# Exponentials of four key tiles computed during the MLP and kept in HBM, maxima by one matmul a unit, w2 re-read per chunk

## The chip, the cores and the metric

The kernel runs on one core of one Trainium2 chip. The metric is the device time of one launch, in microseconds; the median of several runs is given, and beside it one execution with the hardware profiler, whose trace is read below. The engines are named as in the profile: PE (TensorE matmuls), PEld (its weight loads), DVE (VectorE), ACT (ScalarE), POOL (GpSimd), SP (SyncE, which here only issues DMAs).

## The reference

One transformer block in parallel form, for 2048 tokens of width 448, all in float32:

```python
xn = layernorm(x)                                   # S, D = 2048, 448
# A: 16 query heads of 28, one shared key and value head
q = (xn @ wq).reshape(S, 16, 28);  k = xn @ wk;  v = xn @ wv
p = softmax(einsum("qhd,kd->hqk", q, k) * 28 ** -0.5)
A = einsum("hqk,kd->qhd", p, v).reshape(S, 448) @ wo
# B: a second layer norm, then an MLP of width 1792
h = gelu(layernorm(xn) @ w1 + b1)                   # tanh form
B = h @ w2 + b2
out = x + A + B
```

## The kernel before

Tokens are taken in 4 chunks of 512 (CW). Projections and MLP work in pairs of fp32r halves: a value is split into a high part and a rest, and three products (high by high, high by rest, rest by high) are added in PSUM.

The kernel has three stages, in one order that is written out by hand (each engine and each DMA queue runs its instructions in that order). 

Stage 1 (`norm_parts`, `q_slot`, `v_slot`): both layer norms, transposes of x, and the projections. Queries go to HBM, a high part in `qd[0]` and the rest in `qd[1]`, as rows of 512 tokens (L407); keys stay in SBUF as `ks` (four blocks of 32 partitions, the high part and the rest twice each). A few of the keys are also kept as `kz`, 32 keys per block.

Stage 2, the MLP: 4 chunks of 14 slots (`mlp1(c, ft)` and, two slots behind, `mlp2`). `mlp1` runs 11 matmuls into a PSUM bank `ph`, then ACT and DVE compute gelu in five instructions (L567 to L571), and the result is split by DVE and POOL into `hh` and `hl`. `mlp2` runs 12 matmuls of 448 columns into four banks (L586). Both halves of w2 (`w2h`, `w2l`) are made in the first chunk and stay in SBUF. MLP results plus x and b2 go to HBM as `ad`.

Stage 3, attention: 16 units, each one of 4 chunks by one of 4 groups of 4 heads. `load_q` brings a unit's queries into a tile `qst` (blocks of 28 partitions). `max_jobs` takes each query's largest score over 32 keys (16 matmuls of 128 columns, 4 DVE reductions, a transpose, and two small DMAs that write the negated maximum into rows 60 and 124 of the query tile, where `ks` holds ones, so that the score matmul subtracts it). Then a unit has 8 steps of two key tiles:

```python
            for i, (kt, h) in enumerate(((k, h) for k in (2 * step, 2 * step + 1) for h in range(2))):
                scores(u, kt, h)
...
            for v, kt in waiting:
                pv(v, kt)
```

`scores` (L697, L699) is a pair of matmuls of 128 keys by 512 queries for two heads into a two-bank tile `s` (three of them), and one exponential of 1024 columns into `p`. `pv` (L706) multiplies the weights `p` by the values, for four heads in four column strips of PE, one step behind the scores. `norm_jobs` normalises a finished unit, with small DMAs through HBM; `o_jobs` multiplies a finished chunk by wo (12 matmuls in each of four steps, L663 to L665) and writes the output. `last_norm` ends the last unit. If a sum of weights lies outside wide limits, a branch at the end recomputes attention with exact maxima; it is not taken here.

SP issues nearly all DMAs, and in program order: a DMA that waits for a semaphore holds those behind it.

Of the kernel before, what the change touches and what calls it, by code (L numbers as in the profile page):

```python
# [18 lines left out]
P = 128  # L19
S, D, H, DH, F = 2048, 448, 16, 28, 1792  # L20
NT = S // P
CT = 4
# [10 lines left out]
PAIRS = 14  # L33
# [4 lines left out]
def block_kernel(ctx, tc, x, wq, wk, wv, wo, w1, b1, w2, b2, out):  # L38
# [18 lines left out]
    qd = [dram.tile([D, S], F32, name=f"qd{i}") for i in range(2)]  # L57

    ks = keep.tile([P, S], F32R, name="ks")
    kz = keep.tile([P, P], F32R, name="kz")  # L60
# [76 lines left out]
    pool.memset(f(kz), 0.0)  # L137
# [231 lines left out]

    def w2_split(s):  # L370
        raw = wl_q.pop(0)
        ab = slice(2 * s, 2 * s + 2)

        act.activation(w2h[:, ab, :], raw, AF.Copy, scale=0.5)
        dve.scalar_tensor_tensor(w2l[:, ab, :], raw, 0.5, f(w2h[:, ab, :]), op0=ALU.mult, op1=ALU.subtract)  # L375
        if s + 2 < NF // 2:
            w2_load(s + 2)

    def q_slot(c, i):
        xh, xl = xts[c, False]  # L380
        cols = slice(c * CW, (c + 1) * CW)
        ms = slice(i * P, (i + 1) * P)
        ps = qpp.tile([P, CW], F32, name="qp")
        for cs in (slice(0, CW // 2), slice(CW // 2, CW)) if c < 2 and i == 0 else (slice(0, CW),):
            proj(ps, lambda b: wah[:, b, ms], lambda b: wal[:, b, ms], xh, xl, cs)

        def evac():
            qe = wqp.tile([P, 2, CW], F32R, name="qe", bufs=5)
            if c in KEPT:
                dve.tensor_mul(ps, ps, ibs[c])  # L390
            act.activation(qe[:, 0, :], ps, AF.Copy)
            vt = None
            if i == 0:
                vt = wqp.tile([32, CW], F32, name="vt", bufs=1)
                act.activation(vt, ps[0:32, :], AF.Copy)

            def low():
                dve.tensor_sub(qe[:, 1, :], ps, f(qe[:, 0, :]))  # L398
                if i == 0:
                    for dst, j in ((32, 0), (0, 1), (64, 1), (96, 0)):  # L400
                        nc.sync.dma_start(f(ks[dst:dst + DH, cols]), f(qe[32:60, j, :]))
                        if c == 0:
                            nc.sync.dma_start(f(kz[dst:dst + DH, :]), f(qe[32:60, j, 0:P]))
                at = slice(64 if i == 0 else 0, P)
                rows = slice(0, 64) if i == 0 else slice(i * P - 64, i * P + 64)
                for j in range(2):
                    nc.sync.dma_start(qd[j][rows, cols], f(qe[at, j, :]))  # L407
            return vt, low
        return evac
# [105 lines left out]
    def load_q(u, blocks=range(4)):  # L515
        c, g = units[u]
        qs = qss[u] = qst[u % 2]
        for b in blocks:
            blk, i = ((1, 0), (2, 0), (0, 1), (3, 1))[b]
            src = qd[i][4 * DH * g:4 * DH * (g + 1), c * CW:(c + 1) * CW].rearrange("(j r) n -> r j n", r=DH)  # L520
            nc.sync.dma_start(f(qs[32 * blk:32 * blk + DH]), src)

    def max_jobs(u, whole=False):
        qs = qss[u]
        mr = keep.tile([P, 4 * CT], F32, name="mr", bufs=2)
        for j in range(4):
            js = slice(CT * j, CT * j + CT)
            if whole:
                mx = keep.tile([P, CT, 4], F32, name="mx")
                for t in range(CT):  # L530
                    for n in range(4):
                        pm = bank([P, CW])
                        pe.matmul(pm, qs[:, j, t * P:(t + 1) * P], ks[:, n * CW:(n + 1) * CW], start=True, stop=True)
                        dve.tensor_reduce(mx[:, t, n:n + 1], pm, axis=AX.X, op=ALU.max)
                dve.tensor_reduce(mr[:, js], mx, axis=AX.X, op=ALU.max)
            else:
                pm = bank([P, CT, P])
                for t in range(CT):
                    pe.matmul(pm[:, t, :], qs[:, j, t * P:(t + 1) * P], kz, start=True, stop=True)  # L539
                dve.tensor_reduce(mr[:, js], pm, axis=AX.X, op=ALU.max)  # L540
            yield
        pm = bank([4 * CT, P])
        pe.transpose(pm, mr, ident)
        mn = keep.tile([4 * CT, 2, P], F32R, name="mn", bufs=2)
        dve.tensor_scalar(mn[:, 0, :], pm, -1.0, 0.0, op0=ALU.mult, op1=ALU.add)
        dve.scalar_tensor_tensor(mn[:, 1, :], pm, -1.0, f(mn[:, 0, :]), op0=ALU.mult, op1=ALU.subtract)
        for row, i in ((60, 0), (124, 1)):
            nc.sync.dma_start(f(qs[row:row + 1, :, :]), f(mn[:, i, :]))
        yield
# [5 lines left out]
    w2h = hp.tile([P, NF, D], F32R, name="w2h", bufs=1)  # L555
    w2l = hp.tile([P, NF, D], F32R, name="w2l", bufs=1)
# [3 lines left out]
    def mlp1(c, ft):  # L560
# [3 lines left out]
        proj(ph, lambda b: w1h[:, b, fs], lambda b: w1l[:, b, fs], yh, yl)  # L564
# [4 lines left out]
        dve.scalar_tensor_tensor(hz, hz, 1.0, hx, op0=ALU.add, op1=ALU.mult)  # L569
        act.activation(hz, hz, AF.Tanh, scale=GELU[1])  # L570
# [7 lines left out]
    def mlp2(c, ft):  # L578
# [4 lines left out]
        terms = ((hh, w2h), (hh, w2l), (hl, w2h))  # L583
        for k in range(CT):
            for i, (h, w) in enumerate(terms):
                pe.matmul(m2[k], h[:, k * P:(k + 1) * P], w[:, ft, :], start=(ft == 0 and i == 0),  # L586
                          stop=(ft == NF - 1 and i == 2))
            if ft == NF - 1:
                t = CT * MLP_ORDER[c] + k
                a = lines.pop(t)  # L590
                dve.tensor_add(a, a, m2[k])  # L591
                nc.sync.dma_start(ad[:, t, :], a)

# [6 lines left out]
    first_max = None  # L600
    for n in range(len(mslots) + 2):
        c, ft = mslots[n] if n < len(mslots) else (NCH, n - len(mslots))
        if 3 <= ft < 11 and ft % 2 and len(KEPT) <= c + 1 < NCH:
# [10 lines left out]
        if (c, ft) == (NCH - 1, 1):  # L614
            clear_q()
        if (c, ft) == (NCH - 1, 3):
            load_q(0)
            first_max = max_jobs(0)
        if n < len(mslots):
            mlp1(c, ft)  # L620
# [4 lines left out]
        if c == NCH - 1 and 6 <= ft < 11:  # L625
            next(first_max)
        if n >= 2:
            mlp2(*mslots[n - 2])
# [6 lines left out]
    clear_q()  # L635
# [66 lines left out]
    def pv(u, kt):  # L702
        if kt == 0:
            pos[u] = op.tile([P, CW], F32, name="po")
        for j in range(4):
            pe.matmul(pos[u][32 * j:32 * j + 32, :], vs[:, kt, :], ps[u, kt, j // 2][:, j % 2, :],  # L706
                      start=(kt == 0), stop=(kt == NT - 1))

    def last_norm(u, po):
# [5 lines left out]
        def blocks(t, h):  # L715
            return t[:, h].rearrange("p (a b) -> p a b", b=32)

# [3 lines left out]
        for i in range(2):  # L721
            h, r = slice(256 * i, 256 * i + 256), slice(8 * i, 8 * i + 8)
            dve.transpose(tr[:, h], po[:, h])
            dve.reciprocal(rc[:, r], blocks(tr, h)[:, :, 0])
            dve.transpose(blocks(rb, h), rc[:, r, None].to_broadcast([P, 8, 32]))
            dve.tensor_mul(on[:, h], po[:, h], rb[:, h])
            pool.tensor_copy(sums[:, u, r], blocks(tr, h)[:, :, 0])
# [9 lines left out]
    def at(u, step, g):  # L737
        side.setdefault((u, step), []).append(g)
# [4 lines left out]

    load_rows_of(0)
    waiting = []
    for u in range(NU):
        c, g = units[u]
        for step in range(NT // 2):
            if step == 0 and u + 1 < NU:
                load_q(u + 1)  # L750
                nexts = max_jobs(u + 1)
            for i, (kt, h) in enumerate(((k, h) for k in (2 * step, 2 * step + 1) for h in range(2))):
                scores(u, kt, h)
                if i == 0:
                    for job in side.pop((u, step), []):
                        next(job, None)
                if i == 1 and 2 <= step < 7 and u + 1 < NU:
                    next(nexts)
            for v, kt in waiting:
                pv(v, kt)  # L760
            if waiting and waiting[-1][1] == NT - 1:
                v = waiting[-1][0]
                job = norm_jobs(v, pos.pop(v))
                next(job)
                at(u, 2, job)
                at(u, 4, job)
                cv, gv = units[v]
                if gv == NG - 1:
                    outs = o_jobs(cv, range(NG))
                    for d in (6, 7, 8, 9):  # L770
                        at(u + d // 8, d % 8, outs)
                    at(u + 1, 2, rows_job(cv + 1))
                if v == NU - 2:
                    outs = o_jobs(NCH - 1, range(NG - 1))
                    for d in (5, 6, 7, 7):
                        at(u, d, outs)
            waiting = [(u, 2 * step), (u, 2 * step + 1)]
    for v, kt in waiting:
        pv(v, kt)
# [14 lines left out]
    with tc.If(outside > 0, preferred_fallthrough_block=False):  # L794
        for u in range(NU):
            c, g = units[u]
            pool.memset(f(qst[u % 2]), 0.0)
            load_q(u)
            for _ in max_jobs(u, True):
                pass  # L800
            for kt in range(NT):
                for h in range(2):
                    scores(u, kt, h)
                pv(u, kt)
# [29 lines left out]
```

## Time and profile before

| | |
|---|---|
| median of 3 runs | 975.1 us (974.23 to 975.5) |
| profiled execution | 976.61 us |
| its span, first to last instruction | 974.8 us |
| PE busy | 937.5 us (96%), 5181 matmuls |
| ACT busy | 645.3 us (66%) |
| DVE busy | 280.8 us (29%) |
| POOL busy | 154.8 us (16%) |
| DMA | 56.61 MB, mean 58 GB/s |
| first MLP matmul, last MLP matmul | about 66 us, about 352 us |
| attention | to about 960.6 us |

A busy PE is not PE at its peak, since matmuls are pipelined and each one's duration includes its passage through the array. Better measures are the spacing of starts and the chain of waits: the work that ended last, followed back from the last instruction, where each piece is shown with its start, its duration and what it was.

### The profile page before, as it was taken

The page shows a single profiled execution, that of the slowest core. Times are in us where ns is not written, and L with a number is a line of the kernel's source. Part 1 is how long each engine was busy: PE and PEld are TensorE (multiplying, and loading weights), DVE is VectorE, ACT ScalarE, POOL GpSimd, SP SyncE. Part 2 cuts the span into 40 slices and gives each one's busy share as a digit, 9 for nine tenths or more (in the row PEclk, how much of TensorE's full clock was granted, in tenths as well). Part 3 has the DMA queues.
Part 4 walks back from the last instruction along what each step waited for, and adds up shares of the span by engine and source line. Part 5 has one row for each costly group of instructions (what it writes and reads, how often), then busy time and mean ns, then how long its engine had stood idle before and what let it go on. Part 6 is the DMA issues. An engine that isn't in the chain of part 4 may idle for free.

```text
span 974.8 us, 13404 instructions
## 1 busy us (share of the span) xinstructions
PE 937.5 (96%) x5181; PEld 586.0 (60%) x5181; DVE 280.8 (29%) x539; ACT 645.3 (66%) x772; POOL 154.8 (16%) x149
## 2 busy tenths in 40 slices
PE   9999999999999979999999999999999999999995
PEld 8878888888888854444445644445644444644442
DVE  7855454353443431111102112111111112111003
ACT  6755443334443346888887688887688888588871
POOL 6434342342243320000000000000000000000000
PEclk9999999999999998999999999999999999999998
DMA  9771202002013050210210410210301201222001
GB/s 279 204 253 38 87 8 76 1 24 63 20 55 70 2 139 8 51 39 13 50 40 22 111 41 16 51 39 12 113 19 45 51 17 35 68 60 50 2 12 41
DMA packets 40256, 56.61 MB, mean 58 GB/s; under 512 B 10234, under 2 KB 26808, under 8 KB 40184
## 3 DMA queue, kind: packets, MB, share of 16 engines
q1 hardware_dynamic: 38776, 55.10, 20.1%
q8 instruction: 42, 0.69, 0.3%
q10 hardware_dynamic: 1408, 0.57, 0.2%
q14 instruction: 30, 0.25, 0.1%
HBM read 39.49 MB, written 14.80 MB: 56 GB/s over the span
## 4 chain that ended last, share of the span: by engine, by line
PE 87%; ACT 6%; DVE 2%; DMA 2%; issue 1%; POOL 0%; SPq 0%; ACTq 0%; DVEq 0%; POOLq 0%
PE po L706 24%; PE s L697 24%; PE m L586 13%; PE ph L173 11%; ACT p L699 5%; PE qp L173 3%; PE mo L539 3%; PE mo L665 1%; PE mo L663 1%; PE mo L664 1%; PE ph L178 1%; PE ph L176 1%; DMA xh<-qd 1%; DMA xl<-in_A_wo_dram 1%; PE qp L297 1%
## 5 line engine op out<-in xcount | busy, mean ns | idle before, releaser
L699 ACT ACTIVATE p<-s 128x1024 f32<-128x1024 f32 x512 | 484.6, 1029 | 127.0 <-PE s L697 127.0
L697 PE MATMUL s<-xh,ks 128*128 128x512 f32 x1024 | 308.9, 423 | 13.2 <-ACT p L699 10.9
L697 PEld LDWEIGHTS s<-xh,ks 128*128 128x128 f32 x1024 | 168.6, 189 | 176.0 <-ACT p L699 155.1
L706 PE MATMUL po<-p,vs 128*32 128x512 f32 x2048 | 247.7, 602 | 0.0
L706 PEld LDWEIGHTS po<-p,vs 128*32 128x32 f32 x2048 | 53.7, 109 | 124.6 <-issue 123.3
L567 ACT ACTIVATE hx<-ph,b1t 128x512 f32<-128x512 f32 x56 | 38.5, 688 | 117.3 <-PE ph L178 114.5
L689 POOL TENSOR_TENSOR otl<-oc,oth 128x512 fp32r<-128x512 f32 x15 | 19.2, 1280 | 559.1 <-DVE oth L688 559.1
L575 POOL TENSOR_TENSOR hl<-hx,hh 128x512 fp32r<-128x512 f32 x56 | 77.5, 1383 | 186.8 <-DVE hh L574 181.4
L540 DVE TENSOR_REDUCE mr<-mo 128x4 f32<-128x512 f32 x64 | 44.2, 691 | 201.4 <-PE mo L539 201.4
L586 PE MATMUL m<-w2l,hh 128*128 128x448 f32 x224 | 82.5, 368 | 0.9 <-DVE w2l L375 0.9
L586 PE MATMUL m<-w2h,hl 128*128 128x448 f32 x224 | 82.0, 366 | 1.0 <-POOL hl L575 1.0
L586 PE MATMUL m<-w2h,hh 128*128 128x448 f32 x224 | 82.4, 368 | 0.0
L569 DVE SCALAR_TENSOR_TENSOR hz<-hz,hx 128x512 f32<-128x512 f32 x56 | 44.5, 794 | 106.8 <-ACT hz L568 106.4
L173 PE MATMUL ph<-xh,w1h 128*128 128x512 f32 x168 | 66.1, 394 | 2.4 <-DVE qe L398 2.4
L570 ACT ACTIVATE hz<-hz 128x512 f32<-128x512 f32 x56 | 35.4, 632 | 48.3 <-DVE hz L569 48.3
L173 PE MATMUL ph<-xl,w1h 128*128 128x512 f32 x168 | 66.2, 394 | 0.0
L173 PE MATMUL ph<-xh,w1l 128*128 128x512 f32 x168 | 66.2, 394 | 0.0
L675 DVE COPY oc<-po 128x512 f32<-128x512 f32 x15 | 10.4, 692 | 146.6 <-PE po L706 146.6
L571 DVE SCALAR_TENSOR_TENSOR hx<-hz,hx 128x512 f32<-128x512 f32 x56 | 39.1, 699 | 43.6 <-ACT hz L570 43.6
L586 PEld LDWEIGHTS m<-w2l,hh 128*128 128x128 f32 x224 | 42.1, 188 | 7.2 <-DVE w2l L375 3.3
L539 PEld LDWEIGHTS mo<-kz,xh 128*128 128x128 f32 x256 | 38.7, 192 | 11.3 <-issue 5.6
L586 PEld LDWEIGHTS m<-w2h,hh 128*128 128x128 f32 x224 | 42.1, 188 | 4.9 <-DVE a L591 0.2
(148 smaller groups left out, 813.7 us busy)
## 6 DMA issues: line engine op xcount, KB each, us to landing
xh<-qd SPq DMA_DIRECT2D x64, 224.0 KB
qd<-qe SPq DMA_DIRECT2D x24, 256.0 KB
a<-in_A_x_dram SPq DMA_DIRECT2D x24, 224.0 KB
tr<-ld SPq DMA_DIRECT2D x60, 64.0 KB
ad<-a SPq DMA_DIRECT2D x16, 224.0 KB
a<-ad SPq DMA_DIRECT2D x16, 224.0 KB
raw<-in_B_w_dram SPq DMA_DIRECT2D x7, 448.0 KB
out_dram<-a SPq DMA_DIRECT2D x14, 224.0 KB
```

The lines of the kernel that those rows point to most:

```text
L173: pe.matmul(ps, w, v, start=(n == 0), stop=False)
L539: pe.matmul(pm[:, t, :], qs[:, j, t * P:(t + 1) * P], kz, start=True, stop=True)
L540: dve.tensor_reduce(mr[:, js], pm, axis=AX.X, op=ALU.max)
L567: act.activation(hx, ph, AF.Identity, bias=b1t[:, ft:ft + 1])
L569: dve.scalar_tensor_tensor(hz, hz, 1.0, hx, op0=ALU.add, op1=ALU.mult)
L570: act.activation(hz, hz, AF.Tanh, scale=GELU[1])
L571: dve.scalar_tensor_tensor(hx, hz, 1.0, hx, op0=ALU.add, op1=ALU.mult)
L575: pool.tensor_sub(hl, hx, f(hh))
L586: pe.matmul(m2[k], h[:, k * P:(k + 1) * P], w[:, ft, :], start=(ft == 0 and i == 0), stop=(ft == NF - 1 and i == 2))
L697: pe.matmul(s[:, i, :], ks[:, kt * P:(kt + 1) * P], qss[u][:, 2 * h + i, :], start=True, stop=True)
L699: act.activation(p, s, AF.Exp, scale=SCALE)
L706: pe.matmul(pos[u][32 * j:32 * j + 32, :], vs[:, kt, :], ps[u, kt, j // 2][:, j % 2, :], start=(kt == 0), stop=(kt == NT - 1))
```

## The change

The exponentials of key tiles 0 to 3 (`STORED`) of every unit are computed during the MLP. In each slot from the third on, `between()` is called five times: once after the fourth `ph` matmul, twice after the two activations that read `ph`, and after the third and fourth token tile of `mlp2`. Each call takes one more item of `aside()`: one score matmul (128 keys, 512 queries of one head) into one of two PSUM banks (`sbank`), one exponential into one of four buffers `e`, and a DMA of 256 KB into HBM (`pd`). The 256 items fill 51 slots.

The maxima of a unit come from one matmul with `kd`, which holds 32 keys once for each of the four heads on a block diagonal, then a DVE transpose in 32 by 32 blocks, a reduction, a negation, a transpose back, a DMA of the result to HBM (`md`), and a DMA from there into the query tile. A unit's strips, queries and maxima are fetched while the unit before it is worked on. In the attention stage the queries and the shift row are loaded a second time, into `qst`.

Memory for this comes from w2: its halves are written to HBM (`wd`) in the first chunk and read back in pairs of slots (896 KB) in the other three, through three buffers.

In attention a step has three pairs of scores and not four (key tiles 4 to 15), and `fetch` brings one stored pair (512 KB) a step into one of 14 buffers, ahead of its use. PV takes the key tiles in the order `WEIGHTED`.

The core of the diff:

```diff
-PAIRS = 14
+PAIRS = 12
+HELD = 14
+STORED = 0, 1, 2, 3
+FRESH = tuple(kt for kt in range(NT) if kt not in STORED)
+WEIGHTED = 0, 1, 4, 5, 6, 2, 7, 8, 9, 3, 10, 11, 12, 13, 14, 15
...
+    md = [dram.tile([4, CW], F32, name=f"md{u}") for u in range(NCH * NG)]
+    pd = [dram.tile([len(STORED), P, 4, CW], F32, name=f"pd{u}") for u in range(NCH * NG)]
+    wd = [dram.tile([P, 2, 2, D], F32, name=f"wd{s}") for s in range(NF // 2)]
...
     def w2_split(s):
         raw = wl_q.pop(0)
-        ab = slice(2 * s, 2 * s + 2)
-
-        act.activation(w2h[:, ab, :], raw, AF.Copy, scale=0.5)
-        dve.scalar_tensor_tensor(w2l[:, ab, :], raw, 0.5, f(w2h[:, ab, :]), op0=ALU.mult, op1=ALU.subtract)
+        t = w2_tile(0, s)
+        act.activation(t[:, :, 0, :], raw, AF.Copy, scale=0.5)
+        dve.scalar_tensor_tensor(t[:, :, 1, :], raw, 0.5, f(t[:, :, 0, :]), op0=ALU.mult, op1=ALU.subtract)
         if s + 2 < NF // 2:
             w2_load(s + 2)
+        nc.sync.dma_start(wd[s], f(t))
...
+    def load_strips(u, qm):
+        c, g = units[u]
         for j in range(4):
...
+            rs = slice(DH * (4 * g + j), DH * (4 * g + j + 1))
+            nc.sync.dma_start(f(qm[32 * j:32 * j + DH, :]), qd[0][rs, c * CW:(c + 1) * CW])
+
+    def load_max(u, qs):
+        nc.sync.dma_start(f(qs[60:61, :, :]), md[u])
...
+    def block_max(pm, tm, keys, qm, dst):
+        pe.matmul(pm, keys, qm, start=True, stop=True)
+        dve.transpose(tm, pm)
+        dve.tensor_reduce(dst, blocks(tm), axis=AX.X, op=ALU.max)
+
+    def shift_rows(u, tm, mr):
+        mn = keep.tile([P, CW // 32], F32R, name="mn", bufs=2)
+        dve.tensor_scalar(mn, mr, -1.0, 0.0, op0=ALU.mult, op1=ALU.add)
+        dve.transpose(blocks(tm), f(mn)[:, :, None].to_broadcast([P, CW // 32, 32]))
+        nc.sync.dma_start(md[u], tm[DH:P:32, :])
...
-        proj(ph, lambda b: w1h[:, b, fs], lambda b: w1l[:, b, fs], yh, yl)
+        for i, _ in enumerate(proj_steps(ph, lambda b: w1h[:, b, fs], lambda b: w1l[:, b, fs], yh, yl)):
+            if i == 3:
+                between()
...
+        between()
+        between()
         act.activation(hz, hz, AF.Tanh, scale=GELU[1])
...
+            if k >= 2:
+                between()
+
+    sides = itertools.count()
+
+    def sbank():
+        return bank([P, CW]) if next(sides) % 2 else sx.tile([P, CW], F32, name="sx")
+
+    def stored(u):
+        for n, kt in enumerate(STORED):
+            for j in range(4):
+                s = sbank()
+                pe.matmul(s, ks[:, kt * P:(kt + 1) * P], qx[u % 2][:, j, :], start=True, stop=True)
+                e = hp.tile([P, CW], F32, name="e", bufs=4)
+                act.activation(e, s, AF.Exp, scale=SCALE)
+                nc.sync.dma_start(pd[u][n, :, j, :], e)
+                yield
+
+    def prepare(u):
+        load_strips(u, qm[u % 2])
+        load_q(u, qx[u % 2])
+        yield
+        mr = keep.tile([P, CW // 32], F32, name="mr", bufs=2)
+        block_max(sbank(), tm, kd, qm[u % 2], mr)
+        shift_rows(u, tm, mr)
+        load_max(u, qx[u % 2])
+        yield
+
+    def aside():
+        for u in range(NU):
+            nexts = prepare(u + 1) if u + 1 < NU else iter(())
+            for i, _ in enumerate(stored(u)):
+                if i in (0, 7):
+                    next(nexts, None)
+                yield
...
+        if n % 2 == 0 and NF <= n + 2 < len(mslots):
+            s = (n + 2) % NF // 2
+            nc.sync.dma_start(f(w2_tile((n + 2) // NF, s)), wd[s])
...
+    def fetch(u, n, h):
+        p = att.tile([P, 2, CW], F32, name="pq", bufs=HELD)
+        nc.sync.dma_start(p, pd[u][n, :, 2 * h:2 * h + 2, :])
+        ps[u, STORED[n], h] = p
...
+    for step in range(PER * NU + 1):
+        if step % PER == 1 and step // PER + 1 < NU:
+            next(load_next(step // PER + 1))
+        if step > 1 and held:
+            fetch(*held.pop(0))
+        for i in range(3):
+            if fresh:
+                scores(*fresh.pop(0))
+            if i == 0:
+                for job in side.pop(step, []):
+                    next(job, None)
+        for u, i in [weighted.pop(0) for _ in range(2 if step else 0)]:
+            pv(u, WEIGHTED[i], i == 0, i == NT - 1)
```

192 lines of the change are left out of this document (94 added, 98 removed).

## The prediction

> **What bounds the kernel now.** I read the stretches by stage first: the MLP, the handover, attention, the last normalisation. Columns: stretch, its length, busy us of PE, PEld, DVE, ACT and POOL with their counts, granted clock, DMA share, GB/s.
>
> ```profile
> core 0: us, PE busy (x) PEld busy (x) DVE busy (x) ACT busy (x) POOL busy (x), PEclk, DMA share, GB/s
> 66.00:352.40 286.40, 284.46 (x1321) 245.34 (x1321) 128.79 (x204) 116.67 (x183) 99.85 (x75) 0.99 0.14 43
> 352.40:374.10 21.70, 14.74 (x62) 6.27 (x61) 4.52 (x5) 11.32 (x12) 0.98 (x1) 0.84 0.63 160
> 374.10:960.60 586.50, 573.49 (x3451) 282.23 (x3447) 91.38 (x181) 473.31 (x500) 19.20 (x15) 1.00 0.15 40
> 960.60:974.80 14.20, 3.46 (x10) 1.44 (x10) 6.22 (x17) 0.00 (x0) 0.38 (x2) 0.76 0.20 71
> ```
>
> The MLP is TensorE alone (284 of 286 us); ScalarE is at 41%, the DMA engines at 14%. In attention PE looks 98% busy, but its busy time includes pipeline depth, so next I read the chain of waits there (start, duration, what), in three places: a plain step, one with an output projection, one with maxima.
>
> ```profile
> 646.02 1.85 PE po L706 x16
> 647.88 0.68 PE s L697 x2
> 648.63 1.03 ACT p L699
> 649.71 0.74 PE s L697 x2
> 650.45 1.85 PE po L706 x16
> ...
> 540.36 1.85 PE po L706 x16
> 542.21 0.67 PE s L697 x2
> 546.71 1.85 PE po L706 x16
> ...
> 554.92 1.14 PE s L697 x4
> 556.06 0.40 PE mo L539 x4
> 557.49 1.85 PE po L706 x16
> ```
>
> A plain step is 650.45 - 646.02 = 4.43 us and is a loop over both engines: first score pair, its exponential, the fourth pair (there are three s buffers, so it waits for that exponential), then the 16 PV matmuls. The step with four maxima matmuls in it runs 557.49 + 1.85 - 554.92 = 4.42: the maxima lie in PE's wait and cost nothing now. The projection step is PE's own work end to end: 546.71 - 540.36 = 6.35 us.
>
> The MLP's slot in the chain, and ScalarE's rows for it (busy, mean ns | idle before):
>
> ```profile
> 278.30 2.43 PE m L586 x12
> 280.73 2.05 PE ph L173 x9
> 283.24 2.43 PE m L586 x12
> ```
>
> ```profile
> L699 ACT ACTIVATE p<-s 128x1024 f32<-128x1024 f32 x512 | 484.6, 1029 | 127.0 <-PE s L697 127.0
> L567 ACT ACTIVATE hx<-ph,b1t 128x512 f32<-128x512 f32 x56 | 38.5, 688 | 117.3 <-PE ph L178 114.5
> L570 ACT ACTIVATE hz<-hz 128x512 f32<-128x512 f32 x56 | 35.4, 632 | 48.3 <-DVE hz L569 48.3
> L418 ACT ACT_TABLE_LOAD x1 | 1.3, 1283 | 4.3 <-DMA kvraw<-in_A_wv_dram 4.3
> L454 ACT ACT_TABLE_LOAD x1 | 1.3, 1283 | 0.0
> ```
>
> A slot is 283.24 - 278.30 = 4.94 us, with no hole. A ph matmul (512 columns) takes 2.05/9 = 0.228 us, an m matmul 2.43/12 = 0.203. Only two table loads exist, the second before the first tanh, so exponentials between tanhs load no table.
>
> **Attention after.** A step has three score pairs, not four: no pair waits for an exponential of its own step, and PE's work is the bound. From the projection step: 6.35 less 12 matmuls at 0.203 (2.44) is 3.91 for four pairs and PV; less one pair (2 x 0.228) it is 3.45 us. ScalarE needs 3 x 0.946 (484.6/512) = 2.84 of that. So 127 steps after the handover give 438 us; the output projections, of which part now fills PE's wait, stand fully on top: 12 x 2.44 + 4 x 9 x 0.203 = 36.6. The tail stays 14.2. Maxima gone: nothing, as shown.
>
> The handover: how transfers queue there.
>
> ```profile
> 351.31 2.14 SPq L592 DMA_DIRECT2D ad<-a  x4
> 353.58 1.69 SPq L644 DMA_DIRECT2D xl<-in_A_wo_dram  x4
> 355.66 1.77 SPq L655 DMA_DIRECT2D a<-ad  x4
> 357.47 3.53 SPq L521 DMA_DIRECT2D xh<-qd  x4
> 367.69 1.09 PE L539 MATMUL mo<-kz,xh 128*128 128x128 f32 x4 [5.15 <-DMA xh<-qd]
> 370.52 3.62 PE L706 MATMUL po<-p,vs 128*32 128x512 f32 x16
> ```
>
> Now PE waits until 367.7 for the queries of unit 1, behind wo and the rows, and its clock falls (PV 3.62 instead of 1.85). After, the queries come later, but the first PV needs stored tiles 0 and 1, four fetches of 512 KB behind the same wo and rows: about 5.5 us at the rates below, ending near 13 to 16 us after the MLP, then a slow PV. I take 19 us to the start of the next step, which leaves the 127 above; bounds 12 (PE does not idle) and 25. After the MLP then: 19 + 438 + 36.6 + 14.2 = 508 us, against 974.8 - 352.4 = 622.4 before. Attention gives 114 us.
>
> **The MLP after, PE's share.** 256 score matmuls and 16 maxima at 0.228: 62 us, no cover, since PE has no hole there. A full slot is 4.94 + 5 x 0.228 = 6.08 us. ScalarE needs five exponentials at 0.63 (bounds 0.47, half of the 0.946, and 0.69 by the biased row) plus 0.69 + 0.68 + 0.63: 5.2 of 6.08, hidden but tight with only two score banks. The start: unit 0's strips, maxima and shift row come through DRAM before the first score at slot 2; with stores of queries still landing to 70 us I take 8 us (0 to 15). By PE alone: 66 + 286.4 + 62 + 8 + 508 = 930 us.
>
> **The MLP after, transfers.** This is the new term. Sizes and issues, then four stretches in which the DMA engines were full (transfers of one kind each), and the small round trip through DRAM:
>
> ```profile
> qd<-qe SPq DMA_DIRECT2D x24, 256.0 KB
> L407 SPq DMA_DIRECT2D qd<-qe x32: 376/522/747, 28.3 to 67.2; - x32
> L521 SPq DMA_DIRECT2D xh<-qd x64: 307/386/511, 289.9 to 880.7; - x64
> ```
>
> ```profile
> 57.00:63.00 6.00, 6.00 (x29) 4.68 (x29) 3.22 (x10) 3.33 (x6) 2.14 (x3) 1.00 1.04 378
> 66.00:69.00 3.00, 3.00 (x9) 2.40 (x10) 0.00 (x0) 0.00 (x0) 0.00 (x0) 0.63 1.00 363
> 353.00:355.00 2.00, 1.63 (x6) 1.05 (x6) 0.11 (x1) 0.91 (x1) 0.38 (x1) 1.00 0.94 310
> 363.00:366.00 3.00, 0.00 (x0) 0.00 (x0) 1.00 (x1) 1.05 (x2) 0.00 (x0) 1.00 0.94 201
> ```
>
> Stores of 128 rows by 2 KB (66 to 69) run at 363 GB/s; loads into blocks of 28 partitions (363 to 366) at 201; a mix of w2 loads and query stores at 378; rows of x and of the result at 310.
> - 256 stores of exponentials, the shape of qd<-qe: 67.1 MB / 363 = 185 us.
> - Query loads for 16 units and one into the attention tile, four each of 28 partitions by 8 KB (224 KB): 15.6 MB / 201 = 78 us.
> - Strips for the maxima, 28 partitions again: 3.7 MB / 201 = 18 us.
> - w2: 21 reloads of 896 KB, seven writes, raw loads: 28 MB / 378 = 74 us.
> - Rows: 8.3 MB / 310 = 27 us.
>
> Together 122.7 MB and 382 us of full DMA engines, where PE's own work over the 51 slots with stores is 51.2 x 6.08 = 311. Only four e buffers stand between: an exponential waits until the store four before it has landed, ScalarE holds gelu behind it, PE stops at its two banks. So the stretch takes at least what the transfers take: +71 us, and 930 + 71 = 1001.
>
> SP issues a unit's 16 stores at 0.52 and 10 loads at 0.39 in some 12 of 24 us, so issue itself is not the bound. Its waits are the open term:
>
> ```profile
> 624.57 0.34 SPq L681 DMA_DIRECT2D ld<-rc  x1
> 626.01 1.71 SPq L684 DMA_DIRECT2D tr<-ld  x4
> L723 DVE STREAM_TRANSPOSE tr<-po 128x256 f32<-128x256 f32 x2 | 0.9, 444 | 4.4 <-PE po L706 4.4
> ```
>
> In each unit SP waits for the maxima on DVE (two transposes of twice 0.44, a reduction of about 0.7) and then, before it may load the shift row, 1.44 us (626.01 - 624.57) or more for its write to land; the stores 8 to 11 queue behind. That is 2 to 6 us a unit of unfed DMA engines if the queue runs dry. Bounds: 0 (backlog covers it; the exponentials have four buffers, one slot's work) and 4 x 16 = 64. I take the lower end, as four buffers of 0.72 us transfer are about 3 us of backlog. The result of the sum is 1001.
>
> One rule weighed: the Trainium skill (DMA: Bandwidth & Descriptors, "Where 436 GB/s comes from") lets the HBM side bind at about 358 GB/s for HBM to SBUF. The row at 57 to 63 us shows 378 moved, so the measurement goes above it. By the page's figure an estimate would be 122.7 MB / 358 = 343 us, 32 above PE, and 962 in all: the other sign, since the page has no slower rate for loads into 28 partitions, where the row shows 201.
>
> **The rivals.**
> (a) Transfers are hidden: 943 us or less. Mechanism: the loads into 28 partitions do not hold up the stores behind them, so everything runs at the flat 378: 122.7/378 = 325 us, 14 above PE's 311, hence 930 + 14 = 944. The Trainium skill's section named above knows flat rates alone and would side with this. For it: 201 GB/s may be the port of few partitions, and the other transfers might pass. Against: 363 to 366 shows 94% of DMA time taken at 201, so a queue behind it stands still, and the query load issued at 357.5 landed only at 367.7, behind two others. It decides for faster when transfers need less than about 355 us in all, that is, with 930 + 44 = 974.
> (b) The queue behind SP's waits and the small count of e buffers let the DMA engines run dry: at 85% use, 382/0.85 = 449 us, +138, 1068 us. For it: a unit has three bursts in front of the stores (w2, strips and queries, the shift row's round trip), and each hole is time lost, as PE has none to give back. Against: the loop of one e buffer is exponential 0.63, issue 0.52, transfer 0.72 (256 KB at 363), landing about 1.1 (1.44 less 0.34 of issue): 3.0 us, and four buffers in it give 0.75 us a store, nearly the engines' own 0.72.
> (c) The step in attention does not fall to 3.45 because the fetches (512 KB a step, 152 GB/s) arrive late: against it are four steps of lead and a DMA share now of 0.15. At 3.9 a step it would add 57 us to any case.
>
> **How the numbers follow.** The forecast, MLP bound by transfers and between 978 and 1045, gets 0.55; (b), with (c) within it, above 1045, 0.17; (a) and what lies between it and the old time, 0.26; 0.02 lie within 0.2% of before (2 us, about what a measurement can tell from no change). So faster 0.26, same 0.02, slower 0.72. The forecast's own range is 978 to 1045; since (a) holds a quarter, the range given goes from 935 to 1062, leaving out about 0.08 below and 0.11 above. The sum is against the profiled execution (span 974.8, 976.6 with what lies around it; the median of the runs is 975.1, 1.5 less), so a span of 1001 stands for about 1001 in the median.
>
> **What would show it.** The MLP from first ph to last m should last 420 to 430 us with a DMA share above 0.85 and ScalarE's idle time before the new exponentials ended by the stores that read e; slots of about 7.5 us. Right in attention: steps of 3.45, no pair waiting for ScalarE, 16 PV matmuls still 1.85. If the MLP's slots are 6.1 us and the DMA share near 0.8, the slow rate of the 28-partition loads did not hold up stores, and (a) is true. If the DMA share is under 0.8 and slots are over 8 us, with SP waiting for the shift row, it is (b). Steps above 3.6 would say that PE was not the whole bound there.

## The result, and the profile after

The changed kernel takes **1122.4 us** in the median (1120.9 to 1130.1) against 975.3 for the kernel before on the same chip: a ratio of **1.152 [1.147, 1.158]**. The forecast was 1001. The sign was right, the size was not: the time lies outside the range of 935 to 1062.

The same view by stages as before (stretch, length, busy us of PE, PEld, DVE, ACT, POOL with their counts, granted clock, DMA share, GB/s), of the changed kernel. The first four rows are its MLP, handover, attention and tail; the last four are smaller stretches inside the MLP.

```profile
core 0: us, PE busy (x) PEld busy (x) DVE busy (x) ACT busy (x) POOL busy (x), PEclk, DMA share, GB/s
66.00:603.20 537.20, 411.35 (x1576) 327.49 (x1576) 157.74 (x262) 248.41 (x439) 104.07 (x79) 0.85 0.72 230
603.20:619.90 16.70, 8.77 (x30) 2.77 (x29) 3.83 (x4) 5.61 (x6) 0.00 (x0) 0.80 1.02 342
619.90:1106.60 486.70, 479.01 (x2970) 220.10 (x2968) 43.51 (x91) 361.43 (x378) 19.25 (x15) 0.99 0.60 181
1106.60:1120.20 13.60, 3.56 (x14) 1.44 (x10) 6.28 (x17) 0.00 (x0) 0.38 (x2) 0.77 0.21 74
...
66.00:100.00 34.00, 19.55 (x64) 14.90 (x64) 10.01 (x14) 8.96 (x15) 8.91 (x7) 0.70 0.59 160
...
314.00:318.00 4.00, 2.72 (x14) 2.12 (x12) 0.69 (x1) 1.12 (x3) 0.00 (x0) 1.00 0.81 157
318.00:326.00 8.00, 3.55 (x8) 2.46 (x9) 2.97 (x5) 2.20 (x4) 1.80 (x2) 0.55 0.85 291
326.00:330.00 4.00, 4.00 (x13) 3.21 (x12) 1.32 (x2) 1.35 (x3) 0.57 (x1) 0.62 0.01 4
```

After the MLP the kernel takes 517.0 us where 508 were forecast, so the loss is in the MLP: 537.2 us where 427 were forecast. Of these PE works 411.35. The same matmuls at full clock are 284.46 + 62 = 346, so **65 us are PE busy beyond that, most of it at a lower clock** (0.85 on average), and **126 us are idle PE** (537.2 - 411.35). Taken over windows of half a microsecond, PE's busy time times the missing share of the clock adds up to 54 of the 65. The forecast had 79 us of idle (8 for the start, 71 for transfers) and no lower clock: 47 + 65 = 112, about the over-run of 110. The DMA engines are busy 0.72 x 537.2 = 387 us, where 382 were forecast. So the price of the transfers held in total; that the engines would work without holes did not.

Who waits, in the changed kernel (engine and line, what it waited for: us in all, times, longest):

```profile
ACT e L623 <- DMA pd<-e: 157.1, 54, 7.6
...
SPq L555 <- DVE tm L554: 33.7, 14, 3.3
SPq L541 <- DMA md<-tm: 32.9, 16, 5.7
```

The new exponentials' group on the page (busy, mean ns | idle before, by what), then such waits in the chain (start, us, what) and one of them in the timeline (start, us, instruction [idle before]):

```profile
L623 ACT ACTIVATE e<-sx 128x512 f32<-128x512 f32 x128 | 77.0, 602 | 114.4 <-DMA pd<-e 81.9
```

```profile
308.43 5.04 DMA pd<-e
...
313.49 0.31 SPq L532
...
313.90 7.61 DMA pd<-e
...
321.59 0.60 ACT e L623
...
331.02 6.41 DMA pd<-e
```

```profile
321.59 0.60 ACT L623 ACTIVATE e<-mo 128x512 f32<-128x512 f32 x1 [6.47 <-DMA pd<-e]
322.24 0.79 PE L621 MATMUL mo<-qx,ks 128*128 128x512 f32 x1 [5.52 <-ACT e L623]
...
327.38 0.51 SPq L555 DMA_DIRECT2D md<-tm  x1
...
329.09 0.25 SPq L541 DMA_DIRECT2D qx<-md  x1
```

An exponential itself takes 0.60 us (0.63 forecast); what holds it is the store. SP has issued a query load (L532), and a store of exponentials stands behind it for 7.61 us. ScalarE cannot write its next `e` (6.47 us idle), PE cannot write its next bank (5.52), the clock falls to 0.55, and PE's first matmul takes 0.79. While PE still crawls, the maxima go through DVE at 324 to 327, SP waits for them and for `md` to land, and from 326 to 330 the DMA engines stand at 0.01: the next stores queue behind SP's wait. In this place the two faults feed each other: a full queue stops PE, and the maxima, whose matmul stands behind the stop (at 323.25 us), come late, which empties the queue.

Attention is as forecast. A step in the chain:

```profile
782.21 1.85 PE po L776 x16
784.06 1.59 PE s L762 x6
785.65 1.85 PE po L776 x16
```

785.65 - 782.21 = 3.44 us (forecast 3.45), and no exponential in it. The 12 us by which the stretch runs over come where the projection of a finished chunk waits for the normalisation's small DMAs, which stand behind the fetches. This happens three times, and after the first two the clock falls to half (PV 3.36 and 2.22 instead of 1.85). By windows of one microsecond PE idles 8 us in the stretch and loses some 5 to the clock. The first of the three:

```profile
731.32 8.85 DMA ld<-rc
...
741.81 2.24 DMA tr<-ld
...
745.47 1.28 POOL otl L754
...
749.25 3.36 PE po L776 x16
```

### The profile page after: what moved, and what is told of

Same layout as the page of the kernel before. It is cut to its first block, busy times and chain, and to the rows that moved or that the text cites. A ratio compares the mean times of both kernels' runs of the same rounds, so it can differ in the third digit from the quotient of the medians.

```text
span 1120.2 us, 14083 instructions
## 1 busy us (share of the span) xinstructions
PE 963.7 (86%) x4925; PEld 602.2 (54%) x4925; DVE 261.3 (23%) x507; ACT 659.4 (59%) x900; POOL 158.2 (14%) x153
## 4 chain that ended last, share of the span: by engine, by line
PE 56%; DMA 25%; ACT 6%; SPq 6%; issue 3%; DVE 3%; POOL 0%; ACTq 0%; DVEq 0%; POOLq 0%
PE po L776 20%; DMA pd<-e 18%; PE s L762 17%; PE ph L180 5%; PE m L602 5%; ACT e L623 3%; DMA ld<-rc 2%; PE qp L180 2%; SPq L532 2%; DMA md<-tm 2%; PE mo L621 1%; PE mo L730 1%; PE sx L621 1%; SPq L538 1%; ACT hz L580 1%
## 5 line engine op out<-in xcount | busy, mean ns | idle before, releaser
L764 ACT ACTIVATE p<-s 128x1024 f32<-128x1024 f32 x384 | 367.0, 1025 | 139.5 <-PE s L762 132.7
L762 PE MATMUL s<-xh,ks 128*128 128x512 f32 x768 | 217.6, 415 | 1.5 <-DVE a L607 0.8
L623 ACT ACTIVATE e<-sx 128x512 f32<-128x512 f32 x128 | 77.0, 602 | 114.4 <-DMA pd<-e 81.9
L602 PE MATMUL m<-w,hh 128*128 128x448 f32 x448 | 141.7, 401 | 0.0
L623 ACT ACTIVATE e<-mo 128x512 f32<-128x512 f32 x128 | 76.9, 601 | 109.9 <-DMA pd<-e 75.2
L621 PE MATMUL mo<-qx,ks 128*128 128x512 f32 x128 | 58.7, 459 | 60.8 <-ACT e L623 35.5
L602 PEld LDWEIGHTS m<-w,hh 128*128 128x128 f32 x448 | 94.5, 212 | 12.9
L621 PE MATMUL sx<-qx,ks 128*128 128x512 f32 x128 | 58.9, 460 | 44.8 <-ACT e L623 31.1
L602 PE MATMUL m<-w,hl 128*128 128x448 f32 x224 | 89.0, 397 | 0.3 <-POOL hl L589 0.3
L776 PE MATMUL po<-pq,vs 128*32 128x512 f32 x512 | 67.7, 612 | 6.5 <-issue 6.5
```

Source lines behind the costliest of these rows:

```text
L602: pe.matmul(m2[k], h[:, k * P:(k + 1) * P], w, start=(ft == 0 and i == 0), stop=(ft == NF - 1 and i == 2))
L621: pe.matmul(s, ks[:, kt * P:(kt + 1) * P], qx[u % 2][:, j, :], start=True, stop=True)
L623: act.activation(e, s, AF.Exp, scale=SCALE)
L762: pe.matmul(s[:, i, :], ks[:, kt * P:(kt + 1) * P], qss[u][:, 2 * h + i, :], start=True, stop=True)
L764: act.activation(p, s, AF.Exp, scale=SCALE)
```

## The experiments

Theory of the first set: exponentials wait for their stores, since four buffers do not cover a burst of loads in front of a store, and PE's clock falls with it. Rivals: the bytes themselves; SP's waits for the maxima (the prediction's hole term); the issue on one queue. Windows run from 66 us to each kernel's last MLP matmul; after the MLP all variants of the changed kernel take 514 to 519 us.

**Only unit 0's exponentials stored, all fetches read these.**

```diff
+                if u == 0:
+                    nc.sync.dma_start(pd[u][n, :, j, :], e)
-        nc.sync.dma_start(p, pd[u][n, :, 2 * h:2 * h + 2, :])
+        nc.sync.dma_start(p, pd[0][n, :, 2 * h:2 * h + 2, :])
```

> Leaves out 240 of the 256 stores of exponentials (units 1 to 15); attention fetches unit 0's instead, so the weights are wrong but every matmul, exponential and fetch is there. Theory A (the stores and what stands in their queue make the loss): the MLP falls from 537 us to PE's own 348 plus the start, 350 to 370, and the whole to 930 to 960 us, with PE's clock back above 0.97 in the MLP. Rival B (the interleaving itself is too tight: two score banks, ScalarE at 5.2 of 6.1 us): the MLP stays above 420 and the whole above 1000.

974.7 us, ratio 0.998 [0.997, 1.000]; MLP 392.1 us, PE busy 359.7. The stores cost 148 us altogether. Even without them the kernel gains nothing: the matmuls added to the MLP and the start take back all that attention gains. 32 us of PE idle (start, late queries and maxima) and 13 of busy time beyond the 346 (some 9 of it at half clock) are left, more than the theory had.

**Twelve buffers for exponentials.**

```diff
-                e = hp.tile([P, CW], F32, name="e", bufs=4)
+                e = hp.tile([P, CW], F32, name="e", bufs=12)
```

> Twelve e buffers instead of four, nothing else. Theory A1 (few buffers: bursts of loads in front of the stores stall ScalarE, PE waits, its clock drops, the DMA engines then run dry): stalls of 6 to 8 us shrink, the DMA share in the MLP rises from 0.75 to above 0.9, the whole falls to 1000 to 1040 us. Theory A2 (the DMA engines are already at what this mix allows): the MLP stays within 20 us of 537, the whole above 1095 us.

1040.2 us, 1.066 [1.061, 1.071]: **82 us of the loss are the four buffers.** MLP 456.2 us at a DMA share of 0.84. SP's waits in this kernel now name the next thing:

```profile
SPq L541 <- DMA md<-tm: 61.4, 16, 6.3
```

The write of the maxima lands behind more queued stores than before (61.4 us of waiting, 32.9 with four buffers).

**w2 not read again; queries and strips loaded for two units alone.** Two amounts of transfers of nearly the same size are left out, at different places.

```diff
-            nc.sync.dma_start(f(w2_tile((n + 2) // NF, s)), wd[s])
+            w2s[(n + 2) // NF, s] = w2s[0, 4 + s % 3]
```

> The second to fourth chunk use w2 tiles left from the first and reload nothing: 21 loads of 896 KB (19.3 of 122.7 MB in the MLP) are left out, so the MLP's values are wrong. Theory A2 (volume): the MLP falls by 19.3/122.7 of its 537, some 85 us, to a whole of about 1035 us. Theory A1 (bursts of queries and small round trips set the stalls): w2 falls into ScalarE's idle part of a slot and was mostly absorbed, so 20 to 50 us less, 1070 to 1100.

```diff
+        if u < 2:
+            load_strips(u, qm[u % 2])
+            load_q(u, qx[u % 2])
```

> As changed, but strips and queries are loaded for the first two units only in the MLP; the other units use those again (14 x 1.15 MB = 16 MB left out, so their stored exponentials are of the wrong queries). By the prediction's price (201 GB/s into blocks of 28 partitions) that is 80 us of full DMA engines, at a flat 378 it is 42; leaving out 19.3 MB of w2 (51 us) gave 26 us. If the stalls follow engine time, half of 80 comes back: 1075 to 1085. If the query loads are the main burst in front of the stores (A1), more than all of it: 1020 to 1050. If a flat rate holds and volume counts, 1095 to 1105.

1095.9 (1.123 [1.118, 1.128]) and 1049.8 (1.076 [1.068, 1.084]). The MLP rows, in the columns above, of the first and then the second:

```profile
66.00:576.30 510.30, 400.63 (x1576) 323.06 (x1576) 157.76 (x263) 249.03 (x439) 104.27 (x80) 0.86 0.63 204
```

```profile
66.00:530.10 464.10, 389.58 (x1576) 312.66 (x1575) 156.66 (x263) 248.10 (x439) 104.25 (x79) 0.92 0.70 231
```

DMA time falls by 387 - 321 = 66 us for 19.3 MB and by 387 - 325 = 62 us for 16 MB, but the kernel gains 26 us from the first and 73 from the second. Total transfer time alone is not what sets the MLP, and that the bytes alone bind is refuted, as it is by the 82 us that buffers gain with the same bytes. The query loads cost more than their transfers. What sets them apart is that they come in one burst ahead of stores and stand in the maxima's path; which of the two costs how much, this pair of runs does not show.

**The change's w2 traffic alone, in the kernel before** (the diff is the w2 part of the change).

> The kernel before with one part of the change alone: w2's halves written to HBM in the first chunk and read back in the other three. 25.7 MB more in 286 us, DMA share in the MLP from 0.14 to about 0.4, SP free most of the time. All theories: hidden, 974 to 982 us. If it costs more than 10 us, a w2 load comes late by itself (three buffers) and part of the loss is this and not the stores.

978.6 us, 1.003 [1.001, 1.005]; MLP 285.2 us at a DMA share of 0.39. By itself this part is hidden.

**Loads of w2, strips and queries issued on ScalarE's queue.**

```diff
-            nc.sync.dma_start(f(w2_tile((n + 2) // NF, s)), wd[s])
+            nc.scalar.dma_start(f(w2_tile((n + 2) // NF, s)), wd[s])
```

> Within the MLP the loads of w2, strips and queries are issued on ScalarE's queue instead of SP's; same bytes. Theory A1 with the queue as its mechanism (stores stand behind loads in one ring and behind SP's issues): stores pass the loads, the whole falls by 50 to 90 us, to 1030 to 1070. Theory A2 (volume of the engines, whichever queue): within 20 us of 1122. ScalarE pays about ten issues of 0.4 us a unit, some 4 us of 33, which is the cost side: if ScalarE is what binds it is slower than 1122.

1116.2, 1.144 [1.140, 1.148]: 6 us. ScalarE's waits for stores fell from 157.1 to 96.7 us, but some 55 us of waits that end at its own loads of strips and queries came instead. So this run alone does not clear the order on one queue. The early chain below does more: there SP issues the same transfers on its one queue in an MLP of 429.7 us, so neither its issue nor its queue by itself bounds the 537.

**The maxima sent three items after the matmul, the shift row loaded three later**, with four buffers and with twelve.

```diff
-                if i in (0, 7):
+                if i in (0, 7, 10, 13):
```

> As changed, but the write of the maxima is issued three stores later (item 10 of a unit) and the load of the shift row three more (item 13), so that SP does not wait in front of stores. SP's waits there are 33.7 us (for DVE) and 32.9 us (for the landing) over 16 units. Theory A1a (these waits leave the DMA engines unfed, and with four e buffers PE stalls behind them): 30 to 60 us less than 1122, DMA share in the MLP up by 0.04 or more. Rival A1b (the four e buffers alone set the stalls; the next burst takes the place of this one): within 12 us of 1122.

> Both: twelve e buffers and the later round trip of the maxima. If the two causes add (A1 with A1a), the DMA share in the MLP rises from the 0.86 of twelve buffers to 0.93 or more, the MLP falls from 456 to about 415, the whole from 1040 to about 1000, which is the 382 us of full engines that the prediction's sum had. If buffers alone matter, it stays within 12 us of 1040. Below 985 would say that the price of the transfers was too high.

1119.3 (1.148 [1.143, 1.153]) and 1040.1 (1.067 [1.062, 1.072]): no gain over the kernels they start from. SP's wait for `md` fell to 6.5 us, but in the first of the two PE now waits for the late shift row:

```profile
PE mo L621 <- DMA qx<-md: 15.7, 5, 9.1
```

The wait was moved. Taking SP's wait away is worth nothing so long as the chain from strips to shift row starts as late as before.

**Twelve buffers, late maxima, and all these loads and the round trip on ScalarE's queue.**

> Twelve e buffers, the round trip of the maxima issued three and six items later, and all loads of the MLP and the round trip on ScalarE's queue, so that they take turns with the stores in the engines and do not stand behind up to twelve of them. With four buffers the other queue gave 6 us. If the latency of the small chain behind the stores is what remains, 985 to 1015; if the engines are full, within 15 us of 1040; ScalarE pays some 4 us a unit for the issues and waits.

1059.8, 1.086 [1.081, 1.092], 20 us slower than twelve buffers, alone or with late maxima: ScalarE's idle time now ends at its own loads.

```profile
ACT e L623 <- DMA qm<-qd: 20.2, 6, 4.0
...
ACT e L623 <- DMA qx<-qd: 13.0, 2, 8.1
```

**The chain started early** (strips half a unit ahead, maxima at item 2, send at 4, shift row at 8), with twelve buffers and with four.

```diff
+        if 0 < u and u + 1 < NU:
+            load_strips(u + 1, qm[(u + 1) % 2])
-                if i in (0, 7):
+                if i in ((0, 4, 6, 10) if u == 0 else (0, 2, 4, 8)):
```

> Twelve e buffers, and the chain of the maxima started early: strips loaded half a unit ahead, the maxima matmul at item 2 and the shift row's load at item 8 of the unit before. In the trace with twelve buffers alone the chain of waits in the MLP is store, strips, maxima, landing of md, load of the shift row. If that chain is what holds the MLP now at 456 us where the transfers need 382, it falls to 400 to 425 us and the whole to 985 to 1010. If the engines are full at a share of 0.86, it stays within 15 us of 1040.

> As changed with four e buffers, and the early chain of the maxima that together with twelve buffers gave 1013. If the two causes add, 27 us less than 1122, about 1095. If the chain only binds once the buffers no longer do, within 10 us of 1122, like the later round trip alone (1119).

1012.8 (1.038 [1.034, 1.042]) and 1078.9 (1.106 [1.102, 1.109]). The MLP row with twelve buffers:

```profile
66.00:495.70 429.70, 370.85 (x1576) 305.15 (x1576) 164.16 (x263) 248.47 (x439) 103.43 (x79) 0.93 0.88 287
```

Against the changed kernel: buffers alone 82 us, early chain alone 43, both 110, which is 15 less than the sum. I had put the early chain with four buffers at 27 us at the most, and was wrong. With both the MLP takes 429.7 us, the 427 of the prediction, at 0.88 x 429.7 = 378 us of DMA time (382). It is not the same 427 inside, and the agreement is in part luck: PE idles 59 us instead of 79, and 24 us are busy time beyond the 346, most of it at a lower clock. This is about the floor that the prediction priced, and it is still slower than before.

**What a wait costs beside itself.** Rivals: the clock costs so much per wait, or in proportion to its length. In the kernel before, PE is made to wait for DVE in every slot (2 extra DVE operations) or in every third (11).

```diff
+        pe.matmul(pz[:, 0:P], ident, ident, start=True, stop=True)
+        dve.tensor_copy(za[:, 0:P], pz[:, 0:P])
+        for i in range(2):
...
+        pe.matmul(pz[:, 0:P], last[:, 0:P], ident, start=True, stop=True)
```

> The kernel before, with a wait put into the MLP in each slot from the third: a small matmul, a copy and two operations on VectorE, a small matmul that reads their result. About 1.5 to 2 us of wait, 54 times, 80 to 110 us in all. Theory C (the clock falls only behind waits of several us and then costs for some 10 us): the granted clock in the MLP stays above 0.97, and PE's busy time grows by no more than the added matmuls (some 15 us); the whole grows by the waits.

> The same with eleven operations on VectorE in every third slot: about 5 to 6 us of wait, 18 times, 90 to 110 us in all. Theory C: after each wait PE runs at half clock for a while, as at 318 to 329 us of the changed kernel; the granted clock in the MLP falls to about 0.85 to 0.9 and PE's busy time there grows by 30 to 60 us beyond the added matmuls, so the whole is that much longer than the sum of waits. Rival (the clock is only low while PE waits): busy time grows by no more than in the short version.

1466.7 (1.503 [1.500, 1.506]) and 1215.3 (1.245 [1.243, 1.248]). The groups of the added matmuls in the two (busy, mean ns | idle before them):

```profile
L573 PE MATMUL pz<-ident,za 128*128 128x128 f32 x108 | 42.9, 501 | 349.9 <-DVE za L571 340.1 <-POOL hl L591 9.8
```

```profile
L573 PE MATMUL pz<-ident,zb 128*128 128x128 f32 x36 | 14.3, 501 | 191.7 <-DVE zb L571 191.7
```

The short waits were not short: gelu's own DVE work stood in front, so they lasted 6.5 us each, and the long ones 10.6 where 5 to 6 were expected. The experiment did not compare what it meant to, and whether a wait of 2 us costs any clock stays untested, but it compares 6.5 us with 10.6. First: 1466.7 - 976.6 = 490 us longer, less 349.9 waiting and 42.9 added matmuls, is 97 us over 54 waits, 1.8 us each. Second: 238.8 - 191.7 - 14.3 = 32.8 over 18, also 1.8 each. So a wait of either length costs its length and 1.8 us more. One wait of the first, by windows:

```profile
203.00:205.00 2.00, 0.00 (x0) 0.00 (x0) 0.79 (x2) 1.24 (x3) 0.00 (x0) 1.00 0.00 0
205.00:206.00 1.00, 0.00 (x0) 0.00 (x0) 0.90 (x2) 0.64 (x1) 0.00 (x0) 0.62 0.00 0
206.00:209.00 3.00, 0.00 (x0) 0.00 (x0) 2.93 (x4) 0.00 (x0) 2.52 (x2) 0.50 0.00 0
209.00:212.00 3.00, 2.84 (x9) 2.58 (x10) 1.10 (x2) 0.00 (x0) 0.00 (x0) 0.50 0.00 0
212.00:216.00 4.00, 4.00 (x20) 3.42 (x18) 0.00 (x0) 0.00 (x1) 0.00 (x0) 0.99 0.00 0
```

The added matmul that ends this wait:

```profile
209.16 0.80 PE L573 MATMUL pz<-ident,za 128*128 128x128 f32 x2 [6.89 <-DVE za L571]
```

PE is idle from 202.3 (209.16 - 6.89). The clock is 0.62 between 205 and 206, so it falls to half some 3 us into the wait, and it stays there until 212, 2.8 us after work began again: 9 matmuls in three microseconds, then 20 in four. The Trainium skill (TensorE: Matmul & The Clock Gate, "Part 1: The HAM clock gate") gives about 3.4 us of idleness before half clock and about as much work before full clock; the trace agrees roughly here, with some 3 and 2.8. It does not in the place of the changed kernel shown above: there PE stood from 316.7 (322.24 - 5.52), the clock fell some 2 us later, and it was back only at 329, 6.8 us after PE had started again. Why it took longer there is not shown.

In windows of half a microsecond the changed kernel's clock falls to half 22 times in the MLP, for 158 us in all, in stretches of about 3.4 us or twice to five times that. This is where the 54 us come from, 2.5 us a time; it stands beside 54 waits of ScalarE for stores (157.1 / 54 = 2.9 us in the mean, the longest 7.6), so not every such wait halves the clock. With twelve buffers it is 14 times and 30 us, with the early chain too 9 and 20.

**What the attention gain was.** A step before was 4.43 us because the fourth score pair waits for an exponential. If only this wait is what the change removes there, the order of PV should remove it as well, without a byte moved. First, in the kernel before, PV of one tile after every two pairs; then after every third pair, of two tiles and of one in turn (`weigh` pops tiles from a list and keeps all later jobs).

```diff
-            for v, kt in waiting:
-                pv(v, kt)
+                if i % 2 and waiting:
+                    pv(*waiting[i // 2])
```

> The kernel before with one order changed: the PV matmuls of one key tile after the second score pair of a step and those of the other after the fourth, where both stood after the fourth. It tests what the change could gain in attention at all: if the 0.52 us by which a step of 4.43 exceeds PE's own 3.91 is the fourth pair's wait for the first exponential, it goes, and one more switch between the two kinds of matmul (about 0.24) comes in its place: a step of about 4.15 to 4.2, 128 steps, 30 to 35 us less, 940 to 948 us. Rival (ScalarE at 3.77 of 4.43 sets it, or each switch costs more than thought): 968 to 985.

```diff
+                if pairs % 3 == 0:
+                    weigh(u, 2 - next(runs) % 2)
```

> The kernel before, with PV after every third pair of scores (two tiles and one tile in turn) where it stood after every fourth. The changed kernel's attention shows three pairs and two tiles in 3.45 us with no wait; with one tile it should be 1.59 + 1.0 = 2.6, under ScalarE's 2.84. So six pairs take about 6.3 us, a unit 33.6 where it was 35.4, and the four maxima matmuls of a step, no longer in a wait, 0.39 in five steps of eight: 1.7 a unit. The whole 960 to 985. It is slower than 985 if runs of one tile leave ScalarE idle.

The first: 985.7, 1.011 [1.007, 1.015], a miss. Its chain:

```profile
643.15 1.13 PE s L697 x4
644.28 0.39 PE mo L539 x4
644.68 1.00 PE po L706 x8
645.67 1.12 PE s L697 x4
646.79 1.00 PE po L706 x8
```

Two half steps are 2 x (1.12 + 1.00) = 4.24 us: no wait, but twice as many changes between score and PV matmuls. Over 127 steps, 0.19 each would be 24 us gained. But the maxima, free while PE waited, now stand in the chain, 0.39 four times in each of 16 units, 25 us. That leaves some 9 of the 10 us lost. A step with a projection had no wait to lose; it went from 6.35 to 6.71 us (from PV at 541.41 to PV at 548.12 in this run's chain), 0.55 worse than counted for it, which over the 12 full ones is 7 of the 9. The second: 970.8, 0.995 [0.993, 0.997], half a per cent faster.

**The same, with the change's one-matmul maxima** (`kd`, the DVE transposes and reduction, the round trip of `md`; no stored exponentials, w2 as before).

```diff
+        pe.matmul(pm, kd, q, start=True, stop=True)
+        dve.transpose(tm, pm)
+        dve.tensor_reduce(mr, blocks(tm), axis=AX.X, op=ALU.max)
```

> The kernel before with PV after every third score pair, as in the run before (971), and with the change's maxima: one matmul a unit, two transposes and a reduction on VectorE, one row through HBM, in place of 16 matmuls. The 16 matmuls and the transpose were 1.7 us of PE a unit outside any wait there: 16 x (1.7 - 0.23) = 23 us less, about 948. The prediction's reading (maxima cost nothing) holds only where PE waits; if it holds here too, 968 to 974. Late strips or the round trip of the maxima would show as PE waiting for the query tile and give more than 971.

**965.2 us, 0.990 [0.987, 0.992]**: one per cent faster than the kernel before, and so faster than both.

```profile
651.77 1.59 PE s L725 x6
653.36 0.41 PE mo L541
653.77 1.00 PE po L734 x8
654.77 1.60 PE s L725 x6
656.37 1.85 PE po L734 x16
```

The maxima are 0.41 us once a unit and not four times, but the gain over the run without them is 5.7 us, not the expected 23. Three us go because the matmul takes 0.41 and not 0.23. Most of the rest is the sign that the expectation named, late strips: PE waits for them in six units, 12.6 us in all, the longest 3.9 (`PE mo L541 <- DMA qm<-qd`), where the run without had one wait for queries, 4.2. By windows of one microsecond, from 352 to 948 us, PE idles 8 us more than there and loses 5 more to the clock, which falls to half after three of these waits in attention.

## Why the prediction was right or wrong

- **Attention step 3.45**: right, 3.44, with no wait for ScalarE. Handover 16.7 (19), tail 13.6 (14.2): right. The projections were 12 us short: the step "stand fully on top" left out their input's round trip behind the new fetches, which leaves PE idle and then at half clock.
- **PE's 62 us in the MLP, without cover**: right; without the stores PE's busy time there was still 359.7 against 284.5, 75 more, some 9 of it at half clock.
- **382 us of transfers**: right, 387, which is 122.7 MB at 317 GB/s of busy engines. By the figure of the Trainium skill (DMA: Bandwidth & Descriptors, "Where 436 GB/s comes from") 343 us were estimated. The measurement lies 44 us above that estimate. Term by term it is less good than in total, which is luck: by the runs above, 240 stores took 183 us (387 - 0.52 x 392.1) where the price of 363 GB/s makes 173, w2's reloads 66 (51 by 378 GB/s), and the queries and strips of 14 units 62 (80 by 201 GB/s). The price of the loads into 28 partitions was too high and made up for the others.
- **"So the stretch takes at least what the transfers take: +71", with the holes at their lower end of 0: this step failed.** It took a lower bound for the value. The engines worked 72% of the stretch. Four `e` buffers cover about 3 us, as the prediction itself said, and a burst of loads holds a store for 5 to 7.6; that was read as cover enough. Twelve buffers and the early chain, at the same bytes, gave 429.7 for 427 (82 us for the first, 110 for both).
- **Missing term: the clock.** The prediction used a falling clock at the handover (PV 3.62) but not in the MLP, where it forecast 71 us of waits. It cost 54 us by windows, of the 65 of busy time beyond full clock.
- **The start**: 34 - 19.55 = 14 us of idle in the first 34, not 8.
- **"Issue itself is not the bound"**: right, since SP issues the same transfers in the 429.7 us. **w2's re-read within the sum of transfers**: right that it overlaps; with the rest it costs 26 us.
- **Rival (b)** was the right kind, with the very signature that the prediction named for it (DMA share under 0.8, slots over 8 us, here 537.2 / 56 = 9.6, SP waiting for the shift row). It was undersized: 85% use for 72%, and no clock. Rival (a) fell, and (c) too, since steps are 3.44.
- **"Maxima gone: nothing"**: right only inside PE's wait. Once the wait goes they stand in the chain, 25 us, as the first reordering showed.

At bottom the change moves PE's work rather than removing it: scores that filled attention reappear in an MLP that had no hole. Only the 0.52 us of waiting in each plain step was there to be won (4.43 less the 3.91 of PE's own work that the prediction took from the projection step), and a change of order wins part of it without 67 MB of stores.

## What to carry to other kernels

When work moves from one stage to another, ask first whether the engine that bounds both is the same; if so only its waits can be won, and an order without the wait is the cheaper trial. A sum of transfer times is a lower bound: what a stretch takes depends on whether the buffers cover the longest burst in front of a store, and on whether the first link of a chain through DRAM starts early enough. Price each expected long wait of PE with its clock as well: here 1.8 us a wait in the test with waits put in, and 2.5 for each fall of the clock in the changed kernel.

## What the runs showed of the hardware

- A wait of 6.5 us and one of 10.6 us cost the same beyond themselves, 1.8 us, in a stream of these matmuls.
- In the changed kernel the clock fell to half 22 times in the MLP, in stretches of about 3.4 us or two to five times that, and after one wait it was back only 6.8 us after PE had started again, where the test took 2.8.
- Small DMAs pay for the queue in front: the write of the maxima, 8 KB, made SP wait up to 6.3 us with twelve store buffers, and the normalisation's load took 8.85 us behind fetches; the prediction's row for such a round trip on idle engines was 1.44.
- Loads with nearly the same engine time (66 and 62 us) were worth 26 and 73 us to the kernel.
